# Weights of 32 columns beside weights of 64: the state products of a gated linear attention without a padded copy of the keys, and a new order of all steps

## The chip, the cores and the metric

The kernel runs on one core of one Trainium2 chip. The metric is the time of one execution on the device in microseconds (us), the median of several runs; lower is better. One launch computes everything, from the inputs in HBM to the output in HBM. The core has a matrix engine (TensorE, PE in the profile; PEld is its loading of weights), a vector engine (DVE), a scalar engine (ACT), a general one (POOL), and a queue engine (SP) which here issues the DMAs.

## The reference, cut to what matters

Two blocks follow one another. The first is an attention with a complex decay per feature, over 4 batches, 8 heads, 768 tokens and 48 features a head:

```python
mag = np.sqrt(a_re * a_re + a_im * a_im)
scale = np.minimum(mag, 0.999) / (mag + 1e-06)
a_re_n, a_im_n = (a_re * scale, a_im * scale)
for t in range(S):
    new_re = ar * S_re - ai * S_im           # ar, ai: a_re_n, a_im_n of token t
    new_im = ar * S_im + ai * S_re
    kv = np.einsum('bhd,bhe->bhde', k[:, :, t], v[:, :, t])
    S_re, S_im = (new_re + kv, new_im)
    y[:, :, t] = np.einsum('bhd,bhde->bhe', q[:, :, t], S_re)
```

The second is a two-layer MLP over the 3072 rows of y (384 wide, 2048 hidden): `h = x @ w_in`, `g = max(h, 0) + alpha * min(h, 0)`, `out = g @ w_out`. Everything is float32.

## The kernel before, in words

**Units.** The attention is cut into 24 units `u`: 4 batches times 6 chunks of 128 tokens. Instead of running token by token, a unit splits each decay into a magnitude and a phase. Nine tasks of `gates` compute them on ACT and DVE and put them into DRAM (`decs`, `phs`). The queries and keys of a unit lie in one tile `KQ` of 96 partitions (48 features, real and imaginary) by 2 x 8 heads x 128 tokens. `unit` rotates them by the phases (L579, L581) and then goes over six levels of doubling distance h = 1, 2, 4, ..., 32 (`LEVELS`). At each level `meet` (L596) multiplies keys of one half of a block with queries of the other half, in matmuls of 96 rows and 32 columns of weights; DVE multiplies the decays on (L637); and masks are applied on ACT (L610) or DVE (L620). `T` holds the decays of a unit in its first 96 partitions, 8 heads x 256.

**The state.** After the last level each key carries the decay up to the end of its half of the chunk. For the state the keys are turned so that tokens lie on partitions. For four heads at a time, four transposes (L708) fill the PSUM tile `ps_kt` with 128 tokens x 4 heads x 96. ACT copies this into `T[:, heads, 0:96]` (L710), over decays that are no longer needed, and copies the first 32 of the 96 columns a second time into `T[:, heads, 96:128]` (L711). So the weights of a head fill 128 columns. Then the products `ps_kv` (L720) follow, keys of 64 tokens times values of 64 tokens: for each of the 8 heads `n`, for each half `j` of the 128 columns, for each half `s` of the tokens, one matmul with 64 rows and 64 columns of weights and 48 moving columns. The result of the column half `j = 64` goes to PSUM partitions 64 to 127; DVE reads only partitions 0 to 95 when it adds it to the state `St` (L731), so what the copied 32 columns produce isn't read. The last chunk of each batch has the first token half alone (16 matmuls rather than 32), as its state is not needed afterwards. The state then meets the queries (L746, 96 rows, 48 columns of weights), and the masked products meet the values `VL` (L760, 64 rows, 48 columns). ACT copies the sum into `T` (L771) and a DMA takes it to DRAM (`ysc`).

**The MLP.** Blocks of 256 tokens come back from `ysc` as `xT`. `features` (L817) and, from the third block on, `two_features` (L839) multiply with `w_in`, 128 rows by 128 columns; ACT and DVE apply alpha (L824, L826, L848 to L854). `outputs` (L867) multiplies with `w_out`; from the third block on `seven` (L957) does it in seven half-size products instead of eight, with sums on DVE between.

**The order.** All tasks are Python generators. The string `ORDER` names, letter by letter, which task goes one step further: A to I are the nine of gates, J the loads of q, k, phases and decays, K the copies of v by halves, L the loads of v, M the pieces of weights from DRAM, N and O their conversion for `w_in` and `w_out`, P to Z and a to m the 24 units, n the loads of x, o the MLP. The order in which the steps are emitted is the order on each engine. The amounts given to `DVE(...)`, `ACT(...)`, `PE(...)` and `DMA(...)` in a `yield` are left from the search that found the string: `step` returns nothing, and rings and due times have no effect on the instructions. All DMAs are issued by SP in the string's order.

Of the kernel before, what the change touches and what calls it, by code (L numbers as in the profile page):

```python
# [19 lines left out]
P = 128  # L20
# [7 lines left out]


ORDER = (  # L30
    "ABMABAAABABAAAAAAABMAAAAAMAAAABABBBJMMNMAAAJABBAAKAAAKJJAAAAAAAABBBABJABBBBBBNMBNPBBBPNPJBJKJKJBJBBB"
    "PNBBBPBBBBBBBBBPPPOOOOJLJCPJJLLKKCPOJLLLMLLLLLLLMLLJJOPOPOPNOPPPPONNPPQCPPPQNQCCCCPPPPPPPPPPQQPQPCNC"
    "CCPPPPPPPPPCQQNCCCCCONCCCQOQCNPCPQQQOJMMJPPLMLLJCNQQNORCJLnLCMLLJJJLCCCLLLLQCQRCRQQCCOQNQQQoooooooLL"
    "LNQQRRQNooQQCCCCCNCooQoOoQRQoCQORCCNRRoNooooooORoQOMJONQQoooooRNNOOQQQQRQQROQOQDQQJLRLLnLJJORoLLoooo"
    "LLDMLRNNoLLLLLLooooJDooDDRoooSoSoRRRRRRRRooooooooDRRoRRoRooooRNNNRDSDoDRoDRDSOooooooooRoDoDRSSRJJJJR"
    "RSNSSRRRRDoooooDSDTOooODSLRRoSSoLMLLMJLJLLLLLooSoDSoOTSNoooooSNoOooSSoSoSNSSSSoSDooToSoSooSTSNoooOOo"
    "oNMLLLLLTTSoTSTDSOoTTSDoooooDoDSOKTNoNNNOSSSTSSTSJJJMJLSDDoooooSoooooDJLSSLoOToNTToooToOoOOoooooTTOT"
    "TToTDDTToooooUTnTTooLLLJJLJLDLLLUooooTDToDDoooLLLoLKDoJJJToTTUooDDoDDDTDJTDDDoooooUoTTUTUTTUUUUoVooo"
    "oooooUoTUUVUTTTTVooooooooUUUEJJLLLJJELLLLLLLLLJoLLooooVoEooooUUoUUUEoEVooooooEoEoUVUoUUUoooooUooooEU"
    "UVVUUVUVVVEEEooooooooVoUoKEUVKVUUUUJKKEUUUUKJJJVEVVooVooooEoooEEooEooVVVooooVVVVVVoWoWooooooVoVooJLL"  # L40
    "LJnWooVooVWoLLLLVWWEVEVEEEWEVWWLLLLLLLLEVWWVJEJoKJoooooooooooVVVWVWVVVELKVVLLLLJLJJLLLJJWoWWEWoooooo"
    "oooXXooEEEoEEoooooooooooooooooWWWWWWWoooWXoEWLLLoEoooooooooooWWooooWWoooXoXWWEEEWEEWoJLLLJoooWXWWWEW"
    "XWWWXYWXLWWLLFYXJLnLJJLoooooooXooooooooooooooXXXXXXoooooFoooooooXXFXXoXXXoXooooooooXoXoXYYooooLLLLLL"
    "LLooXXYYXooXYXYYLYooooXooooXFYFooooooXXXXYXYXFYoFYXXXLXLJLJJJLJLLLFooooooooYYoJooooooooooFoooooYYYFF"
    "YooYYooYYoJJLLLJLLJLoZoYooZooYooooFFoooFoYooYYFZoooFFLLooooooooooZooooZZYZYZYFZZYFYFYoooFZYYYZYZYYFo"
    "YooFFYooooooooooFFLLYJJJLooZooooooZZoooooooooooLnFLLFLJLLLJFooLJLLLLZaaFooooooZZoooZFaoFFZZoooooooaF"
    "FoZZZoZFFFoooooooZoooZooaaoooZoZoZZaaZFFFooFJJaoaaZooooooooooooZZZaZZZaZZaoooooooZaoaooabooooooooooo"
    "oooaaooabbZLLZLGJJLLJLJLLGLLLLLaaaoaaooaGooaoooooooJoboaoooaGoobGabaaaJJabbaLKKKoGbGoooooooooooobbbo"
    "ooGGooooGGooooboooooooooababaaGbaGGbGabaLaooooooooocoobLLJJGnKLoooooooooLoLLooobbooocbLLLLLJbbGGGoob"
    "ocooooooLLLKboboboooGGoboooocboooooobbccboocbGbGooooooocccGGoobboooobbbbooooooooooooGcGGKJGGGobcbcbo"  # L50
    "ocbJLJbbLLLJJLocccoooooooooooGooooccGcccocccGdGcoooooooooooocococoocooccoooGGGGcJLLLLLLLLLLdGcocGcoo"
    "oooooodoodooocccddcJJJcdcooooooooooooooooddLLccLHLcJJJLLLJLLdoLdHLLnoooooooodKLLLdddoddooooooooooooo"
    "ooddodddddooHeddoooeodooooodedoHdoooooooooooededdddeeoHddHooooooooeHeeoooHoooddoooooooooooooooddoeee"
    "oddoKJJJJddLLLJeJLLLJJJJLLLeoeoooooooooeHooooHooooooooooffHHooooeeeLJJLLLLLooooooHHHHHHHfooeeooeeeeo"
    "oooooeeoooooooooeoeoooeeeoeHHHfoHeHgefeoooooeeefeHeeKHooofofeeoJJHffoooooooonofHLJLLLLLLLHHooooooooo"
    "offfgoLLJLJJJLLLoofffooooooogHoLooooffoofHHfooooHHHoooooooooofffffoofoofoogoHooooHooooffooooofHHfffH"
    "ffHohhogooooooffgffgffofofhfgogooooooooooooooooggIJJLLLLLLLLJJJIJJgLLLLLLggIgoggIooooooIooooooooooog"
    "goghgIoggogoghIoogooooooogooIoogoogoghhgIhgghIhgoIooohhoooooooooioooooooohogIoIoghggghghhgIggLLLLJJn"
    "hhoooooooooooiLLLLLJLLLLLLJJooohhIhIhhIoooohhhIIihooooooooihoooooooooooooiIhooooooooooooooooooohhJoo"
    "oiiiihhohihIIIohihoooooooJhhihhihihLoohIIiooooooooooiihooooooooooooooiioihILLLoooIiiiijJJLLLJJLLLJji"  # L60
    "iJLLLLLIoiooiooiIiooioiIjiioIIIIIoIooooooooooIIIoiIoooooojiijijiijJIojjjjoooooooooooooooooooijjjjiio"
    "oiijJnJJJLLLLJLLojooooooooooooooooojjjjjjjkkjooooooooojjooojookooooooojoojoookookjkoooookkoooooooooo"
    "oojJJLLLLLLLLLjjoooooookoooooooooojookoooooookooojjjjkjkjjjkLjjkooooooooolkkoLLJJJJJooooookkkokkkook"
    "kooookokkooooolloookooklkllkkkkkloooollooooooooooolJLLLLLLLLLLJLLooooooooooloooooooooklkklkkkklkkLLL"
    "LLnlllooLLLJJLLooooooooooooooollolllloolllooooooolooolmmolloLLLLLoooooloooololmmlooooooooooolooooooo"
    "olmlmlmomomooooooooomoooooooooomoooolmlmlmooooomLLLLLLmomoooooooooLLLLoooooommoooommllmmmmmllLLLLooo"
    "oommoooooomooomooommmmmmmmmomooooooooooommmoooooooooooonoooooooooooooooooooooooooooooooooooooooooooo"
    "oooooooooooooooooooooooooooooooooooooooooooooooooooooooooooooooooooooooooooooooooooooooooooooooooooo"
    "oooooooooooooooooooooooooooooooooooooooooooooooooooooooooooooooooooooooooooooooooooooooooooooooo")

# [27 lines left out]
def kernel(  # L98
# [32 lines left out]
    nc = tc.nc  # L131
    B, HP, _, D, S = q.shape
# [5 lines left out]
    D2 = 2 * D  # L138
    HC = P // 2
# [46 lines left out]
    for h in (16, 32):  # L186
        by_row[h] = []
        for m in range(HC // h):
            t = next(column)
# [373 lines left out]
    def unit(u):  # L563
# [21 lines left out]
        def meet(h, shared, at, keys, queries, *after, takes=()):  # L585

            e = yield PE(0.28, *after, *[("met", h, u - 1)] * (u > 0), takes=takes, mode=1, n=16)
            if not shared:
                shared.append(ps.tile([P, 2, HP, HC // 2], F32, tag="lv", name="ps_lv", bufs=2))
            t = shared[0][:, at]  # L590
            for p in range(4):
                for i in range(2):
                    n = 4 * i + p
                    for g in range(2):
                        j = HC // 2 * g
                        nc.tensor.matmul(t[64 * i + j:64 * i + j + HC // 2, p], lhsT=keys(n, g),  # L596
                                         rhs=queries(n, g), start=True, stop=True)
            done["met", h, u] = e
            return e
# [48 lines left out]
        for visit in VISITS:  # L648
            ready = []
            for h in visit:  # L650
# [29 lines left out]
                if h != visit[-1]:  # L680
                    k_ = yield DVE(2 * H * HC, w, *[("decays", u)] * (h == 1))
                    T = L["T"]
                    step(h, WQ if h == 1 else None)
            tiles, shared = [], []
            for at, (h, keys, queries, held, slot, w) in enumerate(ready):
                e = yield from meet(h, shared, at, keys, queries, w, k_, takes=() if at else (R["lv"],))
# [8 lines left out]
            if visit[0] in pairs:  # L695
                e = yield from mask_both(visit, shared[0], e)
            else:
                for h, ta, e in tiles:
                    e = yield from mask_out(h, ta, e)
# [4 lines left out]
        for i in range(2):  # L704
            e = yield PE(0.333, k_, takes=(R["misc"],), n=2)
            t = ps.tile([P, HP, D2], F32, tag="misc", name="ps_kt")
            for p in range(4):
                nc.tensor.transpose(t[:, p], KQ[:, 1, 4 * i + p], ident[:D2, :D2])  # L708
            e = yield ACT(HP * P + 80, e, ("decays", u))
            nc.scalar.copy(T[:, 4 * i:4 * (i + 1), 0:D2], t)  # L710
            nc.scalar.copy(T[:, 4 * i:4 * (i + 1), D2:P], t[:, :, 0:P - D2])  # L711
            R["misc"].put(e)
        e = yield PE(0.72, e, ("values", u), *[("state", u - 1)] * (u > 0), takes=(R["misc"],) if last else (R["misc"], R["lv"]), mode=2, n=16 if last else 32)
        V = L["V"]
        kv = [ps.tile([P, H, D], F32, tag=tag, name="ps_kv", bufs=n) for tag, n in (("misc", 1), ("lv", 2))[:2 - last]]
        for n in range(H):
            for j in range(0, P, HC):
                for s in range(1 if last else 2):
                    rows = slice(HC * s, HC * (s + 1))
                    nc.tensor.matmul(kv[s][j:j + HC, n], lhsT=T[rows, n, j:j + HC],  # L720
                                     rhs=V[rows, n // 2, (n % 2) * D:(n % 2 + 1) * D], start=True, stop=True)
        ek = e
        states = [state.pop(b)]
# [15 lines left out]
        for s in range(2):  # L739
            before, known = states[s]  # L740
            e = yield PE(0.47, q_, known, takes=() if s else (R["y"],), mode=1, n=8)
# [3 lines left out]
            for n in range(H):  # L745
                nc.tensor.matmul(Y[64 * (n % 2):64 * (n % 2) + D, n // 4, n // 2 % 2, HC * s:HC * (s + 1)],  # L746
                                 lhsT=before[:, n], rhs=KQ[:, 0, n, HC * s:HC * (s + 1)],
# [3 lines left out]
        for s in range(2):  # L751
            for part in range(2):
                e = yield PE(0.335, ("V", u), e, *(made if not (s or part) else ()), mode=2, n=12)
# [14 lines left out]
        for e_ in range(2):  # L768
            t = yield ACT(4 * P, e)
# [4 lines left out]
        for e_ in range(2):  # L774
            t = yield DMA(98, ends[e_], ("state", u))
# [128 lines left out]
    for m, f, c, n in blocks:  # L904
        if m < FIRST:
            i = place[m, f, c][0]
# [236 lines left out]
```

## Time and profile before

| what | value |
|---|---|
| three runs | 762.91, 760.21, 762.88 us |
| median | 762.88 us |
| profiled execution | 765.08 us, of it 763.4 us span from first to last instruction |
| instructions | 26774 |
| TensorE matmuls busy | 674.9 us (88%) in 11728 records |
| DVE busy | 605.4 us (79%) |
| ACT busy | 487.6 us (64%) |
| POOL busy | 13.1 us (2%) |
| DMA | 130.61 MB, 171 GB/s on average |
| granted TensorE clock | 0.998 |

How to read the profile's rows: a group is a line of the code, an engine, an operation and what it writes and reads (out<-in), with the number of records, the busy time, the mean of one in ns, and the idle time of the engine ahead of these records with what ended it. For TensorE a form such as 96*32 means 96 rows and 32 columns of weights. A float32 matmul leaves two records of the matmul and two of the weight load. Matmuls are pipelined, many are in flight at once, and so the mean of one is not what one costs; the distances between starts are. In a timeline each row is a group of neighbouring records: start, length, engine and line, how many. "Idle before" counts only time in which the engine had nothing at all in flight.

### The profile page before, as it was taken

The numbers are of one execution on the slowest core, as the hardware profiler recorded it, in microseconds if no ns is written. First come the engines' busy times: TensorE is split into PE (matmuls) and PEld (weight loads), VectorE is DVE, ScalarE is ACT, GpSimd is POOL, SyncE is SP. The second block draws the span as 40 slices with busy tenths as digits, with TensorE's granted clock in tenths as the row PEclk, the third lists the DMA queues.
The fourth block names the chain that finished last, engine by engine and source line by source line (L and its number), as shares of the span: only waits on it lengthen the run. The fifth ranks groups of instructions, "written<-read, shape, count | busy, mean of one in ns | idle before, by whom it ended". The sixth has DMA issues, their size and how long they took to land.

```text
span 763.4 us, 26774 instructions
## 1 busy us (share of the span) xinstructions
PE 674.9 (88%) x11728; PEld 581.2 (76%) x11728; DVE 605.4 (79%) x798; ACT 487.6 (64%) x886; POOL 13.1 (2%) x48
## 2 busy tenths in 40 slices
PE   0024578999999999999999999999999999999998
PEld 0024456776767888888888889888888988889987
DVE  7889889998999799898986898888996765742323
ACT  8868888985658576946693666756584544453330
POOL 5000000000000000000000000000000000000000
PEclk9999999999999999999999999999999999999999
DMA  9999989979677936787668854865745743421000
GB/s 257 273 258 230 267 236 274 232 216 245 192 194 201 254 83 140 210 223 187 177 170 210 234 123 102 227 188 135 185 129 171 183 104 81 112 43 53 1 21 21
DMA packets 177180, 130.61 MB, mean 171 GB/s; under 512 B 66280, under 2 KB 168424, under 8 KB 176616
## 3 DMA queue, kind: packets, MB, share of 16 engines
q1 hardware_dynamic: 177064, 128.91, 64.3%
q8 instruction: 92, 1.51, 0.9%
q14 instruction: 24, 0.20, 0.1%
HBM read 100.52 MB, written 35.42 MB: 178 GB/s over the span
## 4 chain that ended last, share of the span: by engine, by line
PE 53%; DMA 16%; DVE 11%; SPq 6%; ACT 4%; issue 2%; DVEq 0%; ACTq 0%
PE ps_h L839 19%; PE ps_o L957 17%; PE ps_lv L596 4%; PE ps_y L760 3%; DVE KQ L637 3%; DMA PP<-phs 3%; PE ps_o L867 3%; DMA T<-decs 2%; PE ps_kv L720 2%; SPq L547 2%; PE ps_y L746 2%; DMA xT<-ysc 2%; DMA shared<-in_w_out_dram 2%; DMA VL<-vsc 2%; PE ps_h L817 1%
## 5 line engine op out<-in xcount | busy, mean ns | idle before, releaser
L839 PE MATMUL ps_h<-xT,w_in_sb 128*128 128x256 f32 x960 | 228.6, 384 | 0.7 <-DVE shared L854 0.6
L839 PEld LDWEIGHTS ps_h<-xT,w_in_sb 128*128 128x128 f32 x960 | 176.9, 190 | 22.6 <-DVE shared L854 0.8
L637 DVE TENSOR_TENSOR KQ<-KQ,T 96x1024 f32<-96x1024 f32 x120 | 145.8, 1215 | 28.6 <-PE ps_lv L596 18.9
L957 PE MATMUL ps_o<-w_out_sb,shared 128*128 128x192 f32 x624 | 111.4, 329 | 0.8 <-ACT top L973 0.4
L854 DVE TENSOR_TENSOR shared<-shared,ps_h 128x512 f32<-128x512 f32 x80 | 54.5, 682 | 68.2 <-ACT shared L852 67.9
L957 PEld LDWEIGHTS ps_o<-w_out_sb,shared 128*128 128x128 f32 x624 | 102.4, 190 | 3.5 <-DVE top L963 0.8
L848 ACT ACTIVATE shared<-ps_h 128x512 f32<-128x512 f32 x80 | 47.7, 596 | 80.6 <-PE ps_h L839 80.2
L957 PE MATMUL ps_o<-shared 128*128 128x192 f32 x448 | 80.3, 331 | 0.7 <-DVE top L963 0.7
L852 ACT ACTIVATE shared<-shared,al 128x256 f32<-128x256 f32 x160 | 74.5, 505 | 1.9
L957 PEld LDWEIGHTS ps_o<-shared 128*128 128x128 f32 x448 | 72.7, 190 | 3.3 <-DVE top L963 1.4
L660 ACT COPY WQ<-KQ 96x1024 f32<-96x1024 f32 x48 | 49.9, 1039 | 33.9 <-DVE KQ L637 33.7
L596 PE MATMUL ps_lv<-WQ 96*32 96x32 f32 x2304 | 34.4, 203 | 38.2 <-DVE WQ L579 26.0
L596 PEld LDWEIGHTS ps_lv<-WQ 96*32 96x32 f32 x2304 | 26.2, 116 | 52.4 <-DVE WQ L579 26.0
L817 PE MATMUL ps_h<-xT,w_in_sb 128*128 128x256 f32 (+1 forms) x240 | 53.3, 357 | 4.5 <-DMA xT<-ysc 4.5
L867 PE MATMUL ps_o<-w_out_sb,shared 128*128 128x384 f32 x128 | 51.3, 509 | 5.6 <-DVE shared L826 4.2
L817 PEld LDWEIGHTS ps_h<-xT,w_in_sb 128*128 128x128 f32 x240 | 41.9, 203 | 16.4 <-DMA xT<-ysc 5.2
L760 PE MATMUL ps_y<-A,VL 64*48 64x64 f32 x2304 | 49.1, 225 | 4.5 <-DMA VL<-vsc 4.4
L610 ACT ACTIVATE A<-ps_lv,columns 128x64 f32<-128x64 f32 x144 | 38.3, 334 | 21.4 <-PE ps_lv L596 21.0
L771 ACT COPY T<-ps_y 48x512 f32<-48x512 f32 x48 | 27.7, 576 | 34.5 <-PE ps_y L760 33.7
L676 ACT COPY W<-KQ 96x512 f32<-96x512 f32 x48 | 30.6, 637 | 29.5 <-DVE KQ L637 29.5
L760 PEld LDWEIGHTS ps_y<-A,VL 64*48 64x48 f32 x2304 | 39.4, 123 | 11.0 <-DMA VL<-vsc 5.8
L596 PE MATMUL ps_lv<-KQ,W 96*32 96x32 f32 x1536 | 23.4, 203 | 15.9 <-ACT W L676 15.8
(108 smaller groups left out, 955.8 us busy)
## 6 DMA issues: line engine op xcount, KB each, us to landing
T<-decs SPq DMA_DIRECT2D x48, 384.0 KB
PP<-phs SPq DMA_DIRECT2D x24, 387.0 KB
KQ<-in_q_dram SPq DMA_DIRECT2D x48, 192.0 KB
phs<-gate SPq DMA_DIRECT2D x14, 577.5 KB
decs<-gate SPq DMA_DIRECT2D x7, 1152.0 KB
KQ<-in_k_dram SPq DMA_DIRECT2D x40, 192.0 KB
vsc<-in_v_dram SPq DMA_DIRECT2D x24, 288.0 KB
VL<-vsc SPq DMA_DIRECT2D x48, 144.0 KB
```

The costliest lines, as they stand in the source:

```text
L596: nc.tensor.matmul(t[64 * i + j:64 * i + j + HC // 2, p], lhsT=keys(n, g), rhs=queries(n, g), start=True, stop=True)
L610: nc.scalar.activation(a[:, :, cols], t[:, :, at:at + name], AF.Copy, scale=s)
L637: nc.vector.tensor_tensor(out=x, in0=x if x0 is None else x0, in1=m, op=ALU.mult)
L660: nc.scalar.copy(z.rearrange("p i n t -> p i (n t)").rearrange("p i (m h) -> p m i h", h=h), bass.AP(tensor=KQ.tensor, offset=KQ.offset + ...
L760: nc.tensor.matmul(o, lhsT=Vp[h][64 * i:64 * i + 64, s, e_ * D:(e_ + 1) * D], rhs=a, start=False, stop=(s == 1 and h == LEVELS[-1]))
L817: nc.tensor.matmul(p, lhsT=w_in_sb[:, f // 2, kk, f % 2 * P:(f % 2 + 1) * P], rhs=x_of[m][:, kk, c * P:(c + n) * P], start=(kk == 0), stop ...
L839: nc.tensor.matmul(p[:, i], lhsT=w_in_sb[:, f // 2, kk, i * P:(i + 1) * P], rhs=x_of[m][:, kk], start=(kk == 0), stop=(kk == NK - 1))
L848: nc.scalar.activation(gt, p, AF.Relu, scale=-1.0)
L852: nc.scalar.activation(some_, some_, AF.Copy, scale=al_1[:, f + i:f + i + 1])
L854: nc.vector.tensor_tensor(out=gt, in0=gt, in1=p, op=ALU.add)
L867: nc.tensor.matmul(sums[0], lhsT=gt, rhs=w_out_sb[:, f], start=(f == start), stop=(f == stop))
L957: nc.tensor.matmul(z, lhsT=a[:, i], rhs=w[:, i], start=i == 0, stop=i == F2 - 1)
```

## The change

Three things change. First, the second copy (L711) is left out, so `T` has keys in 96 columns a head and the amount in its `yield` is smaller (which has no effect by itself). Second, the loop over column halves takes the columns 0 to 63 and then 64 to 95 instead of 64 to 127: the second matmul has weights of 64 rows and 32 columns, and writes PSUM partitions 64 to 95 alone. The number of matmuls and their sequence stay: heads, then column halves, then token halves. Third, the string `ORDER` is another permutation of the same 3896 letters, found by a search which took transfers to be longer; each letter is as frequent as before.

```diff
 ORDER = (
-    "ABMABAAABABAAAAAAABMAAAAAMAAAABABBBJMMNMAAAJABBAAKAAAKJJAAAAAAAABBBABJABBBBBBNMBNPBBBPNPJBJKJKJBJBBB"
...
+    "ABAAAABJBABAAAAAAAAAAAAAAABAAABAABBBMKMJMMMJAJBBAAAAAAAAAAMLJBBOAAABAABBBOOBNOBBBBBBBBPPOPMJJJJJBBBB"
...
             for p in range(4):
                 nc.tensor.transpose(t[:, p], KQ[:, 1, 4 * i + p], ident[:D2, :D2])
-            e = yield ACT(HP * P + 80, e, ("decays", u))
+            e = yield ACT(HP * D2, e, ("decays", u))
             nc.scalar.copy(T[:, 4 * i:4 * (i + 1), 0:D2], t)
-            nc.scalar.copy(T[:, 4 * i:4 * (i + 1), D2:P], t[:, :, 0:P - D2])
             R["misc"].put(e)
...
         for n in range(H):
-            for j in range(0, P, HC):
+            for cols in (slice(0, HC), slice(HC, D2)):
                 for s in range(1 if last else 2):
                     rows = slice(HC * s, HC * (s + 1))
-                    nc.tensor.matmul(kv[s][j:j + HC, n], lhsT=T[rows, n, j:j + HC],
+                    nc.tensor.matmul(kv[s][cols, n], lhsT=T[rows, n, cols],
                                      rhs=V[rows, n // 2, (n % 2) * D:(n % 2 + 1) * D], start=True, stop=True)
```

More of the change, by code (lines that the diff above doesn't have):

```diff
@@ L30 @@
 ORDER = (
-    "ABMABAAABABAAAAAAABMAAAAAMAAAABABBBJMMNMAAAJABBAAKAAAKJJAAAAAAAABBBABJABBBBBBNMBNPBBBPNPJBJKJKJBJBBB"
[L32 to L65, printed above, removed]
@@ L66 @@
-    "olmlmlmomomooooooooomoooooooooomoooolmlmlmooooomLLLLLLmomoooooooooLLLLoooooommoooommllmmmmmllLLLLooo"
-    "oommoooooomooomooommmmmmmmmomooooooooooommmoooooooooooonoooooooooooooooooooooooooooooooooooooooooooo"
+    "ABAAAABJBABAAAAAAAAAAAAAAABAAABAABBBMKMJMMMJAJBBAAAAAAAAAAMLJBBOAAABAABBBOOBNOBBBBBBBBPPOPMJJJJJBBBB"
+    "BBBBBBBBPBNBBLBONPNJLLJOPPPNOCJJCKKOPPPPONNMPPPPQPCNPPQQCCPQPQQPPCQPCQQPPPPPPPPCKKMQQQPCPCNCCCKONCPP"
+    "CCCCCPCPOOOJLLLLLLLLJJLJLLNNNCCCJMMPPPPPQPPPPLMCCLnJQROQRMJLLLLLLCLCCLQCCQNNCCLLLLLooCCoQQoCooQQOQNN"
@@ new lines @@
+    "QQQoooCOQCCooQooooQNRNoCCoQQoooORRORQQNROROOoCMDQROOoRQQNNoooooNNQQQQRQQRoRQQLJJQQJJLoooooLJNRoRoooo"
+    "RNonDDDRRRDORooDRRRRRooJJRRoRDDoSooSRRRooooRDooDNoooooDRoRoooooSoRRoooDLLLJoDSNoDSSRooSNSoLMLLLOOooo"
+    "SNDoSooooooDLLLLDDDLRJMSRRRSNRoooooORMJLLJLRRSSoSOSSooooNoJLNOoooooooNSSSSooooooSSSSSSSNTToLJJLLLMLT"
+    "ooSooSTOoSTDSTTSTDoDOSTONoNNooooTTDLLLJLLLSOSSoSoSSTSToDSSDJJMJJSSLoTooToONTooDLDLTNooOoOOOooTTOTnJJ"
+    "oooDTLLLLJJLLooooDTTooUoooUDTTooooTToUooDTDKJLoLLJLLLooTJoUTUUTDUUToUDTDoDDoooooDooDDDDUTTVTVToooooo"
@@ new lines @@
+    "UTTTTUUTTTVTKEUUooooooUooooooJJUooooooooUUoEEoUUUUEooVooEoooooVUUEEoVoooooUooUUooUoULLLLLLLLLLKLKEVV"
+    "UUEVUEVUoEVEoVEVLLLJJJJJEoooooooUUUUVUVUUUULLLJLVEVoooooooJJooooEWEEoooooWLKKLLKJKLooooEooVVoooooooo"
+    "WnWVVoooWWEVEVWEVVVVVoooooooVVoVoVVEVooVWWVooWLLLLLLLJEEJJEEEooVVooooooVWoVVWVVWWEVooVWLLVLVLLLLXXEE"
+    "WWEJJJJJLLLLJoEooooooooooLLLLJoooooWWEEWoWooWoWWWEoEEoooooooWWooWooooooXoWWoooWoWWWWEEXooWXWEooooWXW"
+    "WWWWWWLLXYXoooXXFJoooooonJLLJLooooooXoooXXooXXXXooooooYoooooooXXXXXXXXooooooXoXoKLLLLJLLFLLLLYoXooFY"
@@ new lines @@
+    "ooXooXoYYXYXXYFFFFXXooooYoooYoooooooooooXYXXXXYXYYYoXXYYFooooooooooooooooooooJooJJLXYYoooYFFYYFooYXo"
+    "LLLJJLLLLLJJJLLLJLLoZooooooYoooZFFYYYYoKLoooFFZoYooYooooZoooooooYZYoYYYoooZYYYZFZFFZZooooYoZFYZYZFYo"
+    "oYZooooooooooFFFKJYYZZaZooooooooFFaLFnJLLLJJJFFooooooooooooFFooooooooZZFZZoZoLLLLLLLLaoFooooooKFFFFZ"
+    "oZoooooooooooFFFoZZoZFooZooooaoooZoFooJLLJLoooKoooFJZaZaoaoZZoaaaZZooooooooooaZZZaZaZZaaZaZaZGZboooo"
+    "oooooobooooooLLbGGaaaaoooobLJJaGGoooooooLooaGJLLLLLLLLJJLLKJJKoooooGGbaoooaaaaoooooooooaooabGooGabaa"
@@ new lines @@
+    "abboooGooGGooGbbooooooooooobGGGoooooooobaaababaooooooooooaaGbbbcLaaJLJLcooonJooooooobbbbbbbbooooGbbo"
+    "oooooobobGcooooooobboocbbbbcccccGooGGbbbooooooooooocooooooooooooGGoooooocLLLLLLLLLLLJJLJGJbbcbcbooGb"
+    "bcccLLbbLLGcoooooooooooooccocccccoocoocccodGGooooooocoooocJJJLLLLJJLLLLJLLLccdGGGGGGGdcGcGGccooooooJ"
+    "oGdoooooooooooooooooocdcdcccedooccccdKJJHJodooooooooooddLLJHoLLLoooooddoddedooodooooooooooenJLLLLLLL"
+    "oooooeJLLLooddeedeHdodododdeeoeodooodoodooooooodooooodHddoeoHddddedHHJHHoooooooooooHHooooooooooooood"
@@ new lines @@
+    "deddddoooHefooooeHeefooooooooooooooooeeeeeoeeeLddLLLJJLLLLLLLLLLHHHHeLJooooooooooefoooeooeoeoffefeee"
+    "fefooHofoHeeooooooeeeeoofHooJJoooooJHeHeJLeeoofoHoogKJJLLoooooooooooooooHHHLLLLLffnJJJLLHHHLLooooHfg"
+    "fgffoooooooooooJLLHHgoooooofggfggfoHoffHHoffoooooooooLHfofooooofooofoHHJHHoffoooofgfooofHgooooffogfH"
+    "fgfffgfooooooooogohhfgfggoooofIhooofIooooIooooooooooooggggIgIIIoooooooKoooooooooooJJLLLLLLLLhhIooooo"
+    "gJLLLLJJLLgoggooooooooooooIhggoogoghghghIhhghIoooooooooooooooohIIgghgghgggJJgggihIIhhhLoLLoooooooooI"
@@ new lines @@
+    "ooooooooohhhoJJJJoooooohhhhhhIIooIIiiooohooooooohoooooooohoooohnhIIiiiihhIoooooooooiiiIioooJJJLLLLLL"
+    "LLLLLLIIIhhoooooooooooooohhhihihhoooihhooooiiiIIooooooooIoooooooiiioooiiiiijihhLLJJLLLLLLLLLLLJJJojo"
+    "oooioooojoooiiooijIiiiiijjiooIIIIooooIoooooooooojIjoooooooJJLLjjIIIkkIjoooooooooooooooooooooooijiiji"
+    "iijjjijoooooooooiLLinLLLJoLJJLLJJLLLLLLLoojjooooojjjjojooooojooojoooooooojjooooooooojjoooooooooojkjj"
+    "jjkjoooooooooooooookjkookkokkokooooooooooooojjkjkjjjkkkkLJLjooooooooooooLjLLJLLJoooookkoookkookkookk"
@@ L68 @@
+    "kloooooookkoooolokkooJJJLLLkLLJJLLJLlkkooooloookooooooookkllllkllommoooooooolklkklkokkolloLklLLkLLLo"
+    "ooooooooonolooolloolllllllooooolooooolollooooooooooJLLLLLLJLooooLLoolmloooooooolomooooooooooooooomll"
+    "llmmlommmoomooooooooooooooooooooolmlmlmLLmllmmLLLlLLLlLLLLLLooooooooooooooommmmmmmmoomoooooooooommoo"
+    "ooomomommmmmmmmmoomoooooooomooooommnoooooooooooooooooooooooooooooooooooooooooooooooooooooooooooooooo"
     "oooooooooooooooooooooooooooooooooooooooooooooooooooooooooooooooooooooooooooooooooooooooooooooooooooo"
```

## The prediction

> **What bounds the kernel now.** I read the page's busy times and slices first, to see which engine is full and when. These are the TensorE line of busy times and its row of the slices, each digit tenths of a slice of 19.1 us:
>
> ```profile
> PE 674.9 (88%) x11728; PEld 581.2 (76%) x11728; DVE 605.4 (79%) x798; ACT 487.6 (64%) x886; POOL 13.1 (2%) x48
> ...
> PE   0024578999999999999999999999999999999998
> ```
>
> TensorE fills up over seven slices and stays full from there. The sums by stage say by how much (length, then busy time of each engine, clock, DMA share, GB/s):
>
> ```profile
> 0.00:133.00 133.00, 56.24 (x1418) 44.63 (x1419) 115.93 (x172) 110.55 (x167) 10.91 (x33) 0.99 0.94 256
> 133.00:703.00 570.00, 562.28 (x10002) 483.74 (x10002) 469.25 (x596) 364.11 (x694) 2.19 (x15) 1.00 0.65 168
> 703.00:763.40 60.40, 56.38 (x312) 52.87 (x310) 20.23 (x31) 12.90 (x27) 0.00 (x0) 1.00 0.04 14
> ```
>
> For the first 133 us the DMA engines are 94% busy, and TensorE idles 76.8 us. From 133 us on it idles 7.7 us in 570: whatever TensorE gains or loses there is added to the time one to one. ACT has 206 us free in the same stretch. So I priced the change on TensorE, from the groups that it touches (instructions | busy us, mean ns | idle before):
>
> ```profile
> L720 PE MATMUL ps_kv<-V,T 64*64 64x48 f32 x1408 | 29.0, 224 | 0.7 <-DMA VL<-in_v_dram 0.5
> L720 PEld LDWEIGHTS ps_kv<-V,T 64*64 64x64 f32 x1408 | 26.0, 138 | 5.6 <-ACT T L711 3.3 <-issue 1.1 <-ACT W L676 0.5
> ...
> L711 ACT COPY T<-ps_kt 128x128 f32<-128x128 f32 x48 | 13.4, 279 | 0.0
> ```
>
> Means of 224 ns say nothing of what a matmul costs, since many overlap: 1408 records in 29.0 us are 21 ns each. 704 matmuls leave 1408 records, two each. I therefore took spacings from the timeline (start, length, group). A group's cost is the distance from its start to the next one's:
>
> ```profile
> 464.03 1.16 PE L720 MATMUL ps_kv<-V,T 64*64 64x48 f32 x64
> 465.12 0.66 PE L746 MATMUL ps_y<-KQ,St 96*48 96x64 f32 x16
> 465.70 0.46 PE L596 MATMUL ps_lv<-WQ 96*32 96x32 f32 x32
> 466.09 0.66 PE L746 MATMUL ps_y<-KQ,St 96*48 96x64 f32 x16
> ```
>
> ```profile
> 303.59 0.55 PE L760 MATMUL ps_y<-A,VL 64*48 64x64 f32 x24
> 304.07 0.46 PE L596 MATMUL ps_lv<-KQ,W 96*32 96x32 f32 x32
> ...
> 307.65 2.75 PE L839 MATMUL ps_h<-xT,w_in_sb 128*128 128x256 f32 x12
> 310.24 2.76 PE L957 MATMUL ps_o<-w_out_sb,shared 128*128 128x192 f32 x16
> ...
> 315.52 0.46 PE L596 MATMUL ps_lv<-WQ 96*32 96x32 f32 x32
> 315.80 0.49 PE L596 MATMUL ps_lv<-KQ 96*32 96x32 f32 x32
> 316.21 2.86 PE L839 MATMUL ps_h<-xT,w_in_sb 128*128 128x256 f32 x12
> ```
>
> ```profile
> 641.65 0.46 PE L596 MATMUL ps_lv<-KQ,W 96*32 96x32 f32 x32
> 642.04 0.89 PE L760 MATMUL ps_y<-A,VL 64*48 64x64 f32 x48
> 642.86 1.35 PE L839 MATMUL ps_h<-xT,w_in_sb 128*128 128x256 f32 x5
> ```
>
> The reader is to see a fixed cost at each change of the weights' shape. L760 takes 0.48 us for 24 records and 0.82 for 48: 14 ns a record, and 0.14 that doesn't depend on the number. L596 takes 0.39 for 32 and 0.69 for 64 (two calls in a row): 9.4 ns a record and 0.09 fixed. Two calls of L596 in a row pay it once, and L839 runs into L957 at 12 x 0.216 = 2.59 us with nothing extra: a new line, tile or PSUM bank costs nothing, a new shape does. By the records' starts, the last matmul of one shape is followed by the first of the next after 126 ns (out of the 96*32 of L596) or 145 to 150 (out of 48 or 64 columns), whatever comes next, and the weight load comes no earlier than that first matmul. Inside one shape, four records start 7 ns apart and the next four some 36 ns after these. L746 into L596 (96 rows both, 48 columns then 32) pays 149 ns too, eleven times. Those matmuls go to column 64 last and to column 0 first, so it isn't a collision of two tiles: the whole array waits for the shape.
>
> **The change part by part.** *Second weights of 32 columns instead of 64 (L717 to L720).* Per head the code issues two matmuls of 64x64 weights (one per half of the tokens) and then two of 64x32: 4 records of one shape, 4 of the other, 16 groups a unit. Today all 64 records have one shape: 1.08 us a unit (1.065 for the last unit of each batch, with 32 records). If 64x32 is a new shape as 96x32 is beside 96x48, every group ends in a change.
> - Group of 64 columns: from below 3 x 7 + 148 = 169 ns (spacing inside four, then the exit of this very line), from above the line of L760 carried to four records, 0.148 + 4 x 0.014 = 204 ns, because weights aren't loaded ahead of a change. I take the middle, 187.
> - Group of 32 columns: from below the line of L596 carried to four, 83 + 4 x 9.5 = 121 ns, from above 204 again. Middle, 162.
> - A head 349 ns, a unit 8 x 0.349 = 2.79 us instead of 1.08: +1.71. Ends: 8 x 0.290 - 1.08 = +1.24 and 8 x 0.408 - 1.08 = +2.18.
> - Last units have two records a group; by the same lines 8 x (0.180 + 0.162) - 1.065 = +1.67 (ends +1.14, +2.20).
> - 20 x 1.71 + 4 x 1.67 = 40.9 us. The blocks at 57 and 92 us lie where TensorE idles, so 3.4 are covered by the late DMAs there: **+37.5 us**. Ends 18 x 1.24 + 4 x 1.14 = 27 and 18 x 2.18 + 4 x 2.20 = 48. Were TensorE idle later too, this would shrink; 7.7 us in all are there.
> Queued behind the longer block is every later matmul in the order; DVE's sum into St (L731) gets its input 1.7 us later, and the next late thing is again TensorE, which has other work in the order meanwhile.
>
> By the Trainium skill, "TensorEngine Tiling (Array Packing)", Key Properties, a change of tiling mode, "not just tile", drains the engine, and Tiling Modes lists 64x64 and 64x32 apart. The trace agrees for the pairs above (126 to 150 ns); 64x64 beside 64x32 it doesn't show. By that rule the sum stands as worked out.
>
> *The copy of L711 goes.* 48 x 0.279 = 13.4 us of ACT, 11.7 of them after 133 us where ACT idles. After 133 us no matmul's wait names it, but weight loads do: those of the product for 2.8 us in 9 times, those of the transposes for 1.8 in 6: some 0.3 each, about one copy. Gain from 0 (the matmuls' row) to 4.6 (the weight loads'); I take the middle, **-2 us**, as both rows are of this very place.
>
> *The order.* The 3896 letters are the same in number, each as often as before. From the diff: loads of q and k (J) first at place 7 instead of 35, the weights' pieces (M) at 36 instead of 2, their conversion (N, O) at 76 and 63 instead of 38 and 118, loads of v (L) at 59 instead of 123. The first unit (P) runs from 86 to 244 instead of 81 to 242, the first MLP step is letter 283 instead of 291, the last unit's last letter 3635 instead of 3655. All 26774 instructions less 48 are still issued, SP's DMA issues among them; every engine sees another permutation. At the start DMA is busy 94% of 133 us: a better order gains at most the other 6%, 8 us. Later it gains at most 7.7 idle us of TensorE, and perhaps some of the 288 changes of shape, each 0.09 to 0.11 us over the normal spacing: a tenth fewer is 3 us. Together at most -19, and I bound a loss alike at +19. Since the letters of start and end shift by under 1% of the whole I take 0.
>
> Sum: +37.5 - 2 = +35.5. The profiled execution took 765.08 us (763.4 span, 1.7 around it), 0.3% above the median of 762.88; I put the sum on the median: **798 us**. Against no change a measurement here tells about 0.5% (the three runs span 0.36%).
>
> **Rivals.** *One: no change of shape is paid* (the 64x32 products run beside the 64x64 ones like today's four quadrants, or the weights are placed as 64 wide, so that the change doesn't do to the array what it seems to). For it: two tiles of 64x64 in other columns overlap now. Against: L746 into L596. Four records then cost 58 ns as now (0.93 us over 16), or 38 for the half with L596's spacing: 8 x 20 = 0.16 us a unit, 3.5 over 22, and 2 from L711: **757, the other side**. It decides once a group takes under 73 ns: today's 67 (1.08 us over 16) plus 2 us over 352 groups.
> By the Trainium skill, "TensorE: Matmul & The Clock Gate", LDWEIGHTS, loading time goes with the columns, so 32 would take half. Here 32 take 112 to 116 ns and 64 take 138: the trace doesn't bear a half out, and the gain is the small one above.
>
> *Two: each group refills more slowly.* L746's first pairs after a change are 87 ns apart. If a lone group always pays that, it is 7 + 87 + 7 + 148 = 249 ns, a unit 4.0 us: 22 x 2.9 = 64, less 2, **825 us**.
>
> *Three: the order matters.* A start that is 12 us later (two DMA landings of some 6 us each, as on the chain) gives **810**; a start and stretch better by as much, **786**.
>
> **How the numbers follow.** Forecast 0.76, rival one 0.11, two 0.06, three 0.07 (both ways together). The predicted time is the first's, 798. Its ends are 763 + 27 - 4.6 = 785 and 763 + 48 = 811; with 8 us of order beside, 777 and 819. I give **778 to 819**, leaving out rivals one and two, 17 in 100. Under rival one 757 is -0.8%, but a start worse by 2 us brings it within 0.5%, so it splits: faster 0.07, same 0.04; slower 0.89 holds the rest.
>
> **What would show it.** Right: L720 in two forms (64*64 and 64*32, 704 records each) in alternating groups of four, 126 to 150 ns between groups; a unit's block 2.3 to 3.3 us instead of 1.09; no L711; TensorE as full as now after the start. The two forms' records could also be few ns apart: then rival one, and the block takes about 1 us. Wrong would also be a first 133 us that came out much shorter or longer, or TensorE idle over 15 us in the full stretch: then the order set the time.

## The result and the profile after

The changed kernel takes 829.94 us (three runs, 825.22 to 832.41), the kernel before 762.88: 1.088 times as long, 95% interval 1.080 to 1.097. The range in the prediction, 778 to 819 us, ended below that.

The profiled execution took 832.4 us, 830.7 of it span. TensorE's busy times, its row of the slices, and the row of its granted clock:

```profile
PE 751.1 (90%) x11728; PEld 634.1 (76%) x11728; DVE 608.2 (73%) x798; ACT 480.5 (58%) x838; POOL 11.9 (1%) x48
...
PE   0034888999999999999999999999999999999998
...
PEclk9999889999999989998999999999999999998999
```

And the sums by stage (length, busy time of PE, PEld, DVE, ACT, POOL, clock, DMA share, GB/s):

```profile
0.00:133.00 133.00, 63.38 (x1253) 48.91 (x1253) 108.61 (x162) 103.56 (x153) 10.48 (x33) 0.95 0.87 244
133.00:703.00 570.00, 564.05 (x9300) 473.39 (x9300) 452.23 (x569) 339.03 (x604) 1.43 (x15) 0.97 0.62 163
```

TensorE is as full as it was, 564 us of 570, and does 9300 records in the stretch where it did 10002: each has become dearer. The row holds a second thing that the prediction hadn't: the clock, 1.00 there before, averages 0.97, and five slices show less than nine tenths. The groups that the change made:

```profile
L719 PE MATMUL ps_kv<-V,T 64*64 64x48 f32 x704 | 64.1, 245 | 0.8 <-ACT T L710 0.8
L719 PE MATMUL ps_kv<-V,T 64*32 64x48 f32 x704 | 55.3, 224 | 0.0
...
L719 PEld LDWEIGHTS ps_kv<-V,T 64*64 64x64 f32 x704 | 39.5, 139 | 18.1 <-ACT T L710 4.2 <-issue 1.6
L719 PEld LDWEIGHTS ps_kv<-V,T 64*32 64x32 f32 x704 | 28.0, 109 | 11.2
```

The same 1408 records keep TensorE busy for 119 us instead of 29. A block in the timeline (a row names its first form alone, both are in it):

```profile
440.81 0.38 PE L838 MATMUL ps_h<-xT,w_in_sb 128*128 128x256 f32 x1
441.12 3.72 PE L719 MATMUL ps_kv<-V,T 64*64 64x48 f32 x64
444.77 0.65 PE L745 MATMUL ps_y<-KQ,St 96*48 96x64 f32 x16
```

From start to next start 3.65 us, where before it was 1.09. Within a block the records repeat every 454 ns, a head:

```
64*64:    0    7   94  101      exit  148
64*32:  249  255  315  322      exit  132
64*64:  454 ...
```

So a group of 64 columns costs 248 ns and one of 32 columns 206 (medians of 160 and 140 groups). The last units, with two records a group, pay 242 and 199.

How the 67 us add up, from the starts of TensorE's records after 133 us, that of before against after: the products take 77.3 us instead of 23.0, **+54.3**. Records that start under half clock are dearer than the same form at full clock: 34 of L838 and L816 with 256 moving columns take 444 ns to the next start instead of 227, that is 7.4 us, and so on through the forms, **+16** outside the products. The other terms are -3 together.

The clock is not spread out, it is halved in windows. Sums over one of these windows and its neighbours (as above):

```profile
384.30:388.15 3.85, 3.85 (x33) 2.76 (x32) 3.85 (x6) 2.15 (x3) 0.00 (x0) 0.88 0.57 143
388.15:394.03 5.88, 5.88 (x91) 4.86 (x90) 4.07 (x6) 1.25 (x2) 0.00 (x0) 0.50 0.88 238
394.03:400.00 5.97, 5.97 (x41) 5.33 (x41) 2.85 (x4) 3.68 (x6) 0.00 (x0) 1.00 0.12 38
```

A block of a last unit starts at 384.3; from 387.2 to 394.0 the clock is 0.50, and back to 1.00 after that. After 133 us there are eight such windows (half windows, in what follows) of 3.41 or 6.83 us before the span's end, 37.5 us in all; seven start 2.7 to 3.8 us behind the start of a block, the eighth behind a wait of TensorE of 2.5 us. In the kernel before there was none between 133 us and the end.

The trace's clock records also say why only a third of the 21 blocks after 133 us has one behind it. Within a run all half windows start whole multiples of 3.413 us apart, so a block doesn't start one; it has to fill enough of a step of this grid. In the three kernels with unbroken blocks of 3.6 us (this one, its repetition and the one in the old order below) each of the nine blocks that covered 3.15 us or more of one step was followed by half clock, and 11 of the 54 others. In the steps ahead of these 20 windows the records leave TensorE idle for 0.0 to 0.2 us.

### The profile page after: what moved, and what is told of

It reads as the page before. It is cut to its first block, busy times and chain, and to the rows that moved or that the text cites. A ratio compares the mean times of both kernels' runs of the same rounds, so it can differ in the third digit from the quotient of the medians.

```text
span 830.7 us, 26710 instructions
## 1 busy us (share of the span) xinstructions
PE 751.1 (90%) x11728; PEld 634.1 (76%) x11728; DVE 608.2 (73%) x798; ACT 480.5 (58%) x838; POOL 11.9 (1%) x48
## 4 chain that ended last, share of the span: by engine, by line
PE 80%; DMA 8%; ACT 5%; DVE 4%; SPq 2%; issue 2%; DVEq 0%; ACTq 0%
PE ps_h L838 25%; PE ps_o L956 20%; PE ps_kv L719 10%; PE ps_lv L596 5%; PE ps_y L759 5%; PE ps_o L866 4%; PE ps_h L816 4%; PE ps_y L745 3%; PE ps_kt L708 2%; DMA shared<-in_w_out_dram 1%; DMA T<-decs 1%; DMA KQ<-in_q_dram 1%; DMA gate<-in_a_im_dram 1%; PE ps_h L956 1%; DMA VL<-in_v_dram 1%
## 5 line engine op out<-in xcount | busy, mean ns | idle before, releaser
L838 PE MATMUL ps_h<-xT,w_in_sb 128*128 128x256 f32 x960 | 236.0, 391 | 0.0
L838 PEld LDWEIGHTS ps_h<-xT,w_in_sb 128*128 128x128 f32 x960 | 180.0, 194 | 23.2
L719 PE MATMUL ps_kv<-V,T 64*32 64x48 f32 (+1 forms) x1408 | 94.2, 235 | 0.8 <-ACT T L710 0.8
L719 PEld LDWEIGHTS ps_kv<-V,T 64*32 64x32 f32 (+1 forms) x1408 | 67.5, 124 | 29.3 <-ACT T L710 4.2
L816 PE MATMUL ps_h<-xT,w_in_sb 128*128 128x256 f32 (+1 forms) x240 | 54.9, 366 | 9.1 <-DMA xT<-ysc 8.7
L816 PEld LDWEIGHTS ps_h<-xT,w_in_sb 128*128 128x128 f32 x240 | 44.3, 214 | 22.4 <-DMA xT<-ysc 8.8
L866 PE MATMUL ps_o<-w_out_sb,shared 128*128 128x384 f32 x128 | 55.1, 540 | 1.2 <-DVE shared L825 0.7
L730 DVE TENSOR_TENSOR St<-St,ps_kv 96x384 f32<-96x384 f32 x44 | 24.1, 548 | 34.7 <-PE ps_kv L719 33.4
```

Of the source, the lines that this page charges most:

```text
L719: nc.tensor.matmul(kv[s][cols, n], lhsT=T[rows, n, cols], rhs=V[rows, n // 2, (n % 2) * D:(n % 2 + 1) * D], start=True, stop=True)
L816: nc.tensor.matmul(p, lhsT=w_in_sb[:, f // 2, kk, f % 2 * P:(f % 2 + 1) * P], rhs=x_of[m][:, kk, c * P:(c + n) * P], start=(kk == 0), stop ...
L838: nc.tensor.matmul(p[:, i], lhsT=w_in_sb[:, f // 2, kk, i * P:(i + 1) * P], rhs=x_of[m][:, kk], start=(kk == 0), stop=(kk == NK - 1))
L866: nc.tensor.matmul(sums[0], lhsT=gt, rhs=w_out_sb[:, f], start=(f == start), stop=(f == stop))
```

## The experiments

Theory A: every change between weights of 64 and 32 columns costs, and the order and the copy's removal cost nothing. Rival B: the new order. Rival C: weights of 32 columns are slow in themselves. The kernel before was run beside each set: 767.3, 764.0, 764.9 and 764.7 us.

**The order alone, and the products alone.** The first kernel takes back the copy and the loop (all of the diff but `ORDER`), the second takes back `ORDER` and nothing else.

> The new order alone: the copy of L711 and weights of 64 columns for both halves are back, as before. Theory A (each change between weights of 64 and of 32 columns costs, 16 times a unit): no such change is left, so the time falls back to 755 to 770 us, and the clock is at 0.99 or more. Theory B (the new order sets the time): it stays above 810 us. Theory C (weights of 32 columns are slow by themselves): as A.

> The new products alone, in the order of before. Theory A: 16 groups of 248 and 205 ns instead of 1.08 us a unit, 22 units x 2.55 us = 56 us, and 10 to 20 us of half clock after the long blocks: 825 to 840 us. Theory B: within 10 us of before, 755 to 773. Theory C: as A.

Measured: the order alone 768.45 us, 1.0012 times before (0.9987 to 1.0038), blocks of 1.06 to 1.18 us, no half clock after 133 us. The products alone in the old order: 836.87 us, 1.089 (1.081 to 1.097), and 31 us of half windows after 133 us. The stretch of the first:

```profile
133.00:703.00 570.00, 556.90 (x10004) 478.15 (x10001) 473.46 (x600) 364.75 (x691) 1.43 (x15) 1.00 0.66 169
```

Record numbers and clock are those of before. Rival B falls: the loss comes with the products.

**Sorted by shape, in three degrees.** The order of the loops is changed, nothing else (the kernel in pairs has 2 in place of both 8):

```diff
-        for n in range(H):
-            for cols in (slice(0, HC), slice(HC, D2)):
+        for n0 in range(0, H, 8):
+            for n, cols in [(n, cols) for cols in (slice(0, HC), slice(HC, D2)) for n in range(n0, n0 + 8)]:
```

> As the changed kernel, but the matmuls of a unit are sorted: all eight heads with 64 columns first, then all eight with 32: one change inside a block instead of 15. Theory A: 248 + 7 x (56 to 94) + 205 + 7 x (35 to 67) ns = 1.1 to 1.6 us a block, 760 to 775 us, clock 0.99 or more. Theory B: above 810. Theory C: 8 x 205 + 8 x 58 = 2.1 us a block, some 785 us.

> As the changed kernel, sorted in pairs of heads: 8 groups of one shape a unit instead of 16 (all heads sorted were 2). Theory A (a change costs its exit and refill, some 0.12 us each): two heads with 64 columns 248 + 118 ns, two with 32 columns 205 + 86, a block of 4 x 0.657 = 2.63 us between 3.63 and 1.87; 22 x 1.55 = 34 us over before, some 800 us, and 0 to 8 more where the clock drops. Rival D (what costs is only that the sorted halves fill two tiles of four, not the change): a block of 1.9 us as with all heads sorted, some 780 us.

All heads sorted: 780.41 us, 1.018 (1.012 to 1.024). In pairs: 795.88, 1.040 (1.037 to 1.043). The block of the sorted kernel and of the one in pairs:

```profile
335.83 1.94 PE L719 MATMUL ps_kv<-V,T 64*64 64x48 f32 x64
337.70 0.46 PE L596 MATMUL ps_lv<-KQ,W 96*32 96x32 f32 x32
```

```profile
339.97 2.69 PE L719 MATMUL ps_kv<-V,T 64*64 64x48 f32 x64
342.59 0.46 PE L596 MATMUL ps_lv<-KQ,W 96*32 96x32 f32 x32
```

16 groups take 3.63 us, 8 take 2.62, 2 take 1.87: the same matmuls, some 0.126 us for each group more. Rival D falls. For the sorted kernel theory A's forecast missed (1.1 to 1.6 us a block, 760 to 775 us); the result is nearer to C's, which the next run rules out. That two groups still take 1.87 rather than 1.08 has another reason, seen in the records: sorted, they start in pairs, 7 and 52 ns apart with 64 columns (7 and 36 with 32), where the block of before had fours, 7, 7, 7 and 36. A tile is here the part of the array that one matmul's weights fill. Of four tiles of 64x64 only two are in use at a time when all weights go to column 0. Half clock after 133 us: none when sorted, 6.8 us in pairs.

**Only 32 columns.** Three matmuls of 32 columns instead of 64 and 32, one shape in the whole block:

```diff
-            for cols in (slice(0, HC), slice(HC, D2)):
+            for cols in (slice(0, 32), slice(32, HC), slice(HC, D2)):
```

> As the changed kernel, but with three matmuls of 32 columns for a head and token half instead of 64 and 32: half as many matmuls again, no copy, one shape in the whole block. Theory A: 24 groups of four at 38 to 58 ns, a block of 0.9 to 1.4 us, 755 to 770 us. Theory B: above 810. Theory C: a group of 32 columns takes its 205 ns anywhere, 24 x 205 = 4.9 us a unit, 22 x 3.8 = 84 us more than before, some 845 us.

The block is what theory A said, with half as many matmuls again:

```profile
349.49 1.21 PE L719 MATMUL ps_kv<-V,T 64*32 64x48 f32 x96
350.62 0.54 PE L596 MATMUL ps_lv<-KQ,W 96*32 96x32 f32 x32
```

After 133 us most blocks take 1.02 to 1.15 us (0.81 in the last units; 1.41 and 5.0 in two, the longer one with a wait of 3.5 us in it), so rival C is out for good. But the kernel took 808.31 us, 1.055 (1.049 to 1.061), where theory A said 755 to 770. The loss isn't in the matmuls of the block. Waits of TensorE's matmuls in this run (for whom, us in total, times, longest):

```profile
PE ps_lv L596 <- issue: 18.3, 10, 3.2
...
PE ps_y L759 <- issue: 6.5, 5, 2.6
...
PE ps_kv L719 <- issue: 3.5, 1, 3.5
```

With two smaller rows these are 33.8 us in which the profile shows nothing that TensorE waits for; the waits of its matmuls have no such row in the kernel before, and one of 2.5 us in the changed one. After 133 us 13 of them are 1.1 to 3.5 us long, nearly all at the small matmuls, and the run's eight half windows there (27 us) each start 1.9 to 4.4 us behind the start of such a wait. What TensorE waited for is in the DMA records. The page names a queue that brings instructions:

```profile
q8 instruction: 98, 1.61, 0.9%
```

That is 98 packets of 16 KB. Each of the 13 waits ends 1.2 to 1.6 us after one of them has landed, so by the timing TensorE's instructions came too late. With so many short matmuls the next 16 KB are needed sooner; that this is why they came late is argued, not shown.

**The copy alone.** The copy is left out, and the second weights have 64 columns all the same: the 32 behind the keys are what lies there, old decays, and zeros in the last 32 partitions.

```diff
+        nc.gpsimd.memset(T[D2:P, :, D2:P], 0.0)
...
-            for cols in (slice(0, HC), slice(HC, D2)):
+            for cols in (slice(0, HC), slice(HC, P)):
```

> The copy of L711 left out as in the change, in the new order, but with second weights of 64 columns: behind the 32 keys stand the 32 columns of T that lie there anyway (old decays, and zeros that POOL writes into the last 32 partitions), and what they produce isn't read. Theory A: one shape of weights, 1.08 us a block, no half clock; only the copy's gain is left, 0 to 4.6 us on 767: 762 to 768. If the copy's removal itself slowed the kernel: above 772.

> The same in the order of before: the copy's removal alone, without its price in shapes and without the new order. Theory A: 762 to 768 us beside 767 for before.

New order 766.27 us, 1.0025 (0.9998 to 1.0053); old order 766.05, 1.0027 (1.0002 to 1.0051). Not a gain, if anything 0.3% the other way; the added memset takes 24 x 324 ns on POOL. After 133 us the weight loads that waited for the copies waited 5.4 us instead of 8.1 in the order alone, and the time didn't follow. This is the change's aim without its price, and it is worth nothing here.

**What halves the clock.** First attempt: cut each block in two from the fourth unit on and move steps of the MLP into the cut.

```diff
         for n in range(H):
+            if n == 4 and u > 2:
+                yield PE(0.36)
```

> The changed kernel, with the products of a unit (from the fourth unit on) cut after four heads and ten later steps of the MLP moved into the cut: the same matmuls and changes of shape, in two blocks of 1.8 us instead of one of 3.6. Theory A with the clock (a block of 3.6 us that hardly works the array lets the clock halve for 3.4 or 6.8 us): no half clock from 133 us on but for single windows, and 10 to 16 us less than the changed kernel's 830 less 1 to 5 for the steps moved: 812 to 822 us. Rival E (the half clock has other causes, it costs nothing or comes with the order): as many half windows as before, 825 us or more.

> The changed kernel with its block cut after four heads from the fourth unit on, and eight later steps of the MLP in the cut; this time these are taken evenly from the whole stretch up to the next unit's products, so that none of the cover right behind the block is lost. Theory A with the clock: the changed kernel's matmuls and changes of shape, but blocks of 1.8 us and no half clock from 133 us on but for single windows: 8 to 16 us below the changed kernel beside it, plus what the cut itself costs, which the next run shows. Rival E (the half clock has other causes): 20 us or more of half windows after 133 us, and no gain.

> The same cut and the same order with the copy and the weights of 64 columns: what the cut costs by itself. Both theories: no half clock after 133 us, and 0 to 10 us over before. The difference to the run with the cut in the changed products is the price of the shapes without the long blocks: by theory A 54 us plus single windows, 54 to 60.

> The changed kernel once more, beside the two cut ones: some 830 us, with 30 to 40 us of half windows after 133 us, nearly all of them within 5 us behind the start of a block of products.

863.50, 896.07, 865.47 and 836.56 us. Theory A's forecasts for the first three missed: cut into blocks of 1.8 us they still had 41, 41 and 51 us of half windows after 133 us, as rival E had it, the most in the control, whose blocks of 0.6 us have no change of shape. In the second and third the moved steps of the MLP stand up to eight letters ahead of the last conversions of weights, so a part of the MLP reads weights ahead of their conversion. These three tell little of what the block does to the clock, as they brought another cause for it: TensorE then waited for ACT and DVE (in the first of the three it was idle for 33 us of the full stretch), and the control lost 100 us itself. In the 3.41 us ahead of each of their half windows TensorE was idle for 0.8 to 3.4 us, where it was 0.0 to 0.2 behind the unbroken blocks. A cut by means of the order changes too much. The changed kernel once more had 41 us of half windows after 133 us, in eight windows, each starting 2.4 to 4.3 us behind the start of a block.

Second attempt, with nothing moved: the block made long without a change of shape, and, separately, dense work put into its middle.

```diff
 # long_padded: copy and 64 columns as before
...
-        for n in range(H):
+        for n in [n for _ in range(4) for n in range(H)]:
 # fill_alt, fill_padded (spare_bank: columns of ps_kv that nothing reads)
...
         for n in range(H):
+            for _ in range(8 * (n == 4)):
+                nc.tensor.matmul(spare_bank, lhsT=ident, rhs=ident, start=True, stop=True)
...
```

> New order, copy and weights of 64 columns, and all products of a unit done four times over (each overwrites the same result): a block of 0.15 + 4 x 0.93 = 3.9 us without a change of shape. Theory A with the clock (any block of about 3.5 us that hardly works the array halves the clock): 20 to 40 us of half windows after 133 us, starting 2 to 4 us behind a block; time 767 + 22 x 2.8 + 10 to 20, 838 to 850 us. Rival F (it is the waits at the changes of shape that halve it): no half clock after 133 us, some 829 us.

> The changed kernel with eight matmuls of 128 x 128 x 128 of the unit matrix in the middle of each block, into columns of PSUM that nothing reads: 16 records of 0.11 us and two changes more, 2.0 us of added work a unit, and two stretches of 1.8 us instead of one of 3.6. Theory A with the clock: at most 8 us of half windows after 133 us; the time is that of its control plus the price of the shapes alone, 54 to 58 us. Rival E or F: 20 us or more of half windows, 70 us over its control.

> Its control: the same eight matmuls in the middle of blocks with the copy and weights of 64 columns, in the new order. All theories: no half clock after 133 us, 767 + 22 x 2.0 = 805 to 812 us.

The long block: 908.4 us instead of 838 to 850, blocks of 3.9 to 10.8 us, 37 us of half windows after 133 us. Its weight loads waited 80.6 us for "issue" (nothing that the profile names), so the blocks weren't the even 3.9 us they were meant to be; 21 of the 23 waits of TensorE of 1 us or more after 133 us end 1.2 to 1.5 us after a packet of instructions has landed. Of its eight half windows there one starts within 4 us of a block's start, where the forecast had them 2 to 4 us behind, and ahead of each TensorE was idle for 1.5 to 2.8 us. It shows half clock without any change of shape, but with idle time, so it says little against rival F.

The filled blocks have no such waits inside. With changes of shape 872.36 us, 1.140 (1.135 to 1.144), without 823.93, 1.078 (1.074 to 1.081). The full stretch of the first, and then of its control:

```profile
133.00:703.00 570.00, 558.91 (x9025) 471.33 (x9024) 433.64 (x546) 328.33 (x581) 1.56 (x16) 1.00 0.60 157
```

```profile
133.00:703.00 570.00, 551.75 (x9668) 474.70 (x9669) 455.10 (x573) 346.81 (x644) 1.44 (x15) 0.99 0.62 163
```

The fill keeps all 16 groups and takes the half clock from 31 to 41 us, in three kernels with unbroken blocks, to 3.4. That window, and the one of the control, stand behind a wait for instructions of 1.5 and 3.1 us, not behind a bare block. So changes of shape alone don't halve it; 3.6 us of them without dense work between do. The difference to the control is 48 us, a little under the 54 expected: the control itself was 12 us over the upper end of its expectation, with one half window of 6.8 us and 11 us of "issue" waits after 133 us, against 6 in the other. By the ratios to before, the products cost 6.2% with the fill (1.140 less 1.078), 47 us, and 8.7% without it (1.088 less 1.001), 67 us. The other 19, uncertain by some 8, are what the clock took; the records gave 16. As the control waits 5 us more than the kernel beside it, the 47 is rather too small and the 19 too large.

By the Trainium skill, "TensorE: Matmul & The Clock Gate", Part 1, the gate passes half of the pulses after a window of some 3.4 us in which the engine wasn't busy. The traces agree with the window (3.41 and 6.83 us) and the half (0.50). But by the records TensorE was never idle in those blocks (0.0 to 0.2 us in the step ahead of each of the 20 windows). What the gate counts as busy isn't told by a record, and no run here shows it directly.

## Why the prediction was wrong

*What bounds the kernel* held: TensorE full after 133 us, every microsecond there on the time.

*The change of shape* was the right mechanism, at the right place: two forms, groups of four, exits of 148 and 132 ns, 16 a unit, slower by far. Rival one is out. Mis-sized was the term of the group. I took 187 ns for 64 columns, with 204 as the upper end, and 162 for 32; measured 248 and 206. A unit came to 2.79 us, measured 3.63, and +37.5 us in all became +54. The step that failed is "3 x 7 + 148", four records in one burst, and the line of L760 for the upper end. In L760 and in the block of before, four records at 7 ns go to four different tiles. The group of the changed kernel has two tiles, so two records start, and the second two, on the same tiles, wait for new weights: 87 ns with 64 columns, 60 with 32. The weight loads bear this out: on one tile the second starts 55 ns after the first with 64 columns and 28 with 32, and the matmul 40 ns behind that load both times. The row with two tiles was L746 (7, 87, 7), and I had it in rival two with 0.06. Its 249 ns for 64 columns was exact, for 32 columns too high; its 825 us came near the result because that excess stood for the clock that it hadn't.

*The clock* was in no term and no rival: 16 us by the records, 19 less a few by the filled pair. The profile of before couldn't show it at such a block, as its blocks took 1.1 us; but it had the mechanism once, 3.4 us of half clock at 130 us, and a block forecast at 2.3 to 3.3 us, or 4.0 under rival two, ought to have been held against that length.

*The copy*: I took -2 us from waits of weight loads; the runs show none. The zero that the matmuls' row gave was right. *The order*: 0, right, 1.0012. *The covered blocks* at the start: the early products grew from 4.3 to 15.3 us by the records, and some 160 records slipped past 133 us, while the other terms together are -3 us: covered for the most part, as taken. But there are three such blocks, at 57, 92 and 115 us, and the prediction counted two. Two smaller slips moved nothing much. For the last units the two lines carried to two records give +1.4 us rather than +1.67 (measured +2.5), 1.2 us in all; and the last unit's last letter is 3634 instead of 3642, counted as the other letters are, not 3635 instead of 3655.

## What to carry to other kernels

Price a group of matmuls by how many different tiles it uses and by what shape comes next, not by its records: one change of the weights' shape put 0.13 to 0.15 us between two starts here, and a group on two tiles another 0.06 to 0.09. If a smaller matmul brings a second shape between larger ones, leave the padding (here it needn't even be copied), or sort by shape (still 1.8% slower than before here). And a long run of such groups can cost a second time, through the clock, in work that has nothing to do with it: after 133 us half clock followed 7 of 21 blocks of 3.6 us, 2 of 21 blocks of 2.6 us, and none of 1.9 us.

## What the runs showed of the hardware that I had not expected

- A change in the number of weight columns alone, 64 to 32 with 64 rows, makes the array wait 148 ns from the last start to the next, and 132 on the way back, as much as the other changes of shape here (126 to 150).
- The two records of a float32 matmul don't follow each other when several tiles are in use: the records start in bursts of six with six tiles, of four with four, of two with two, as if a first pass went over all tiles and then a second.
- TensorE without a gap in its records for 3.6 us can lose half its clock for the next 3.4 or 6.8 us; eight dense matmuls in between took the half clock from 31 to 41 us to 3.4. The windows start on a fixed grid of 3.413 us.
- 96 short matmul records a block instead of 64, at the same block time, brought 33.8 us of waits that the profile calls "issue"; those of 1 us and more after 133 us end 1.2 to 1.6 us after 16 KB of instructions have landed.
